# A linear-attention and feed-forward kernel: v loaded in long rows with its ones written by GpSimd, and an order planned for later landings

## The chip, the cores and the metric

The kernel runs on 1 core of one Trainium2 chip. The metric is device time in microseconds, the median of several executions. TensorE (PE) does the matmuls, VectorE (DVE), ScalarE (ACT) and GpSimd (POOL) the rest, and the queue of SyncE (SP) issues most transfers.

## The reference

The inputs are q, k, v of 8 batches x 8 heads x 576 positions x 64, float32, a projection `w_phi` (64 x 128), and the weights of two feed-forward parts, which arrive as float64 and are converted on the chip. What is computed, for each head:

```
phi(x) = [exp(p), exp(-p)]   with p = x @ w_phi - max|x @ w_phi|     (256 features)
kv = phi(k)^T @ v ,  z = sum over positions of phi(k)
attention = (phi(q) @ kv) / (phi(q) @ z + 1e-6)
```

The heads are then joined to x (8 x 576 x 512). The first feed-forward part mixes each position with the one before it (`mu`), and gives sigmoid(xr @ w_r) * (relu(xk @ w_k)^2 @ w_v). The second gives (sigmoid(causal convolution of 5 taps) * (x @ w_val)) @ w_out.

## The kernel before

**Attention.** The 64 pairs of batch and head are taken in 16 rounds n of four heads each; a round is two steps, so there are 32 steps j. In each step two heads (`ab` = 0, 1) go through: projection of q and k on TensorE (`q_proj`, `k_proj`, L615); the largest absolute value and its subtraction on VectorE (L621, L623); exponentials on ScalarE, for q behind a transposition (`turn`, L680, L684); the sums of kv (`kv`, L721); the numerators (`num`, L755); the scaling by the reciprocal of the denominator, on GpSimd and VectorE (`scale`, L772 to L781); and the transposition back (`back`, L795), after which each round is stored to the scratch tensor xs. The last 64 of the 576 positions (the tails) are treated once in a round for all heads.

The z sums come free with kv: v lies in SBUF with 65 columns for each head and block of 128 positions, the 65th a column of ones. Two buffers, `vts[0]` and `vts[1]`, take turns. Their ones are written once, at the start (L576); the load of round n (`load_v`, L599) writes the 64 columns between them, 16 pieces of 256 bytes for each partition, and two small transfers bring the tails. All three go through SP (`load`, L391).

**Conversion of the weights.** 28 pieces of weights are loaded as float64 bits, narrowed to float32 by ScalarE and VectorE (`narrow`, L411 to L425), combined into the seven products of a Strassen scheme, and split by GpSimd into a high and a low part (`part_two`, L463 and L457). The parts of w_k stay in SBUF. All the others go into one of two staging buffers ("ql", shown as dd in the trace) and from there to the scratch tensor ws in HBM; the next cast into a buffer waits until the store from it has landed. This work is spread over the attention steps (`convert`, from FROM to TO).

**Feed-forward parts.** Behind the attention `moe` runs the two parts batch by batch with matmuls of 128x128 against 288 columns (L897), fetching the weights from ws in units (`fetch_unit`, L903), 1 MB each as a rule.

**What sets the order.** The order of the instructions is worked out at build time by a planner, `Order` (the class before the helper functions of durations). Every task has an engine, an estimated duration, what it reads and writes, and a due time in units of a step (the table `T`: `load_v=-1.8` means 1.8 steps ahead of the step itself). For each engine the planner goes through its tasks in the order of due times and takes the first that can start as soon as the engine is free, or, if there is none, the one that can start earliest. A transfer is reckoned to be done DMA_START + bytes / DMA_RATE + DMA_END after it is issued (and behind the transfers before it); what reads it cannot start in the plan before that. For TensorE, tasks of the same array shape are preferred to a due time of EARLY steps ahead. PORT is added where GpSimd and VectorE both work on SBUF. On the chip each engine then runs its list in order, and waits on semaphores where something isn't ready.

Of the kernel before, what the change touches and what calls it, by code (L numbers as in the profile page):

```python
# [25 lines left out]
def pattern(bits):  # L26
# [3 lines left out]
LEAST, MOST = pattern((896 + 128) << 20), pattern(((1150 + 128) << 20) | 0xFFFFF)  # L30


T = dict(load_q=-1.89, load_k=-2.75, load_v=-1.8, tails=-1.0, q_proj=-1.5, k_proj=-1.05, turn=-0.6, sums=-0.5,
         num=0.4, back=1.4, finish=1.9, convert=1.09)
FROM, TO = 1, 27

LAST = ("pj", "qp", "kv")

AFTER_PE = 0.2
AFTER = 0.08  # L40
SAME = 0.04
PORT = 0.28
TAIL = {"ACT": 0.1, "DVE": 0.08, "POOL": 0.05}
DMA_START = 1.3
DMA_END = 1.0
DMA_RATE = 350e3


KV = 0.117
ENTER = {"rows": 0.2, "columns": 0.14, "all": 0.15}  # L50
SOON, EARLY = 0.6, 0.8
SPLIT, FORK_R = 8, False


# [80 lines left out]
class Order:  # L135
# [6 lines left out]
    def add(self, eng, dur, fn, r=(), w=(), new=(), at=None, dma=0, split="all"):  # L142
        t = {"eng": eng, "dur": dur, "fn": fn, "deps": set(), "at": self.now if at is None else at,
             "id": len(self.tasks), "new": list(new), "dma": dma, "end": None, "split": split,
             "bufs": set()}
        t["port"] = eng == "POOL" or eng == "DVE" and dur > 0.3 and not any(
            isinstance(x, Buf) and x.tag in self.banks.most for x in itertools.chain(r, w))
        for x in r:
            t["deps"].update(self.last_write.get(x, ()))
        for x in w:  # L150
            t["deps"].update(self.reads.pop(x, ()))
            t["deps"].update(self.last_write.get(x, ()))
        for x in r:
            self.reads.setdefault(x, []).append(t["id"])
        for x in w:
            self.last_write[x] = [t["id"]]
        for b in new:
            self.queue.setdefault(b.tag, []).append((b, t["id"]))
        for x in itertools.chain(r, w):
            b = x[0] if isinstance(x, tuple) else x  # L160
            if isinstance(b, Buf):
                b.users.append(t["id"])
                t["bufs"].add(b)
        t["deps"].discard(t["id"])
        self.tasks.append(t)

    def run(self):
# [44 lines left out]
        while left:  # L212
# [36 lines left out]
            if t["port"]:  # L249
                other = busy.get("POOL" if t["eng"] == "DVE" else "DVE", 0.0)  # L250
                if at < other - 0.05:
                    t["dur"] += PORT
                    if t["eng"] == "DVE":
                        free["POOL"] += PORT
                        busy["POOL"] += PORT
                busy[t["eng"]] = at + t["dur"]
            free[t["eng"]] = at + t["dur"] - TAIL.get(t["eng"], 0.0)
            t["end"] = at + t["dur"]
            if t["dma"]:
                dma_free = max(dma_free, at + DMA_START) + t["dma"] / DMA_RATE  # L260
                t["end"] = dma_free + DMA_END
            todo[t["eng"]].remove(t)
# [30 lines left out]
def build(ctx, tc, qt, kt, vv, wphi, mu, wk, wr, wv, wval, cw, wout, out):  # L293
    nc = tc.nc
# [30 lines left out]
    for i, side in enumerate(("left", "right")):  # L325
        p = sides[i].enter_context(tc.tile_pool(name=f"s{i}", bufs=1, space=bass.MemoryType.PSUM, side=side))
# [14 lines left out]
    add = G.add  # L341
# [4 lines left out]
    def view(page, off, shape, dtype=F32, own=F32):  # L346
        n = 1
        for k in shape[1:]:
            n *= k
        a, names = pages[page][:, off:off + n], "abcd"[:len(shape) - 1]  # L350
        if len(names) > 1:
            a = a.rearrange(f"p ({' '.join(names)}) -> p {' '.join(names)}", **dict(zip(names, shape[1:])))
        return a if dtype == own else a.bitcast(dtype)
# [34 lines left out]
    def load(dst, src, nbytes, r=(), w=(), new=(), at=None, by="SP"):  # L388

        q = {"SP": nc.sync, "ACT": nc.scalar}[by]  # L390
        add(by, 0.62 if by == "SP" else 0.1, lambda: q.dma_start(out=dst(), in_=src()), r=r, w=w, new=new, at=at,  # L391
            dma=nbytes)
# [166 lines left out]
    vts = [view(*PLACE[f"v{i}0"], [128, 2048]) for i in range(2)]  # L559
    vtok = [Buf(f"v{i}", lambda i=i: vts[i]) for i in range(2)]  # L560
# [10 lines left out]
        load(lambda a=a: wph[64 * a:64 * a + 64], lambda: wphi, 32768, w=[("wph", a)], by="ACT")  # L571
    G.now = -5.0
    for i in range(2):
        def ones(t=vts[i]):
            nc.gpsimd.memset(t[:, 1040:1300], 0.0)
            nc.gpsimd.memset(t[:, 0:1040].rearrange("p (k x) -> p k x", x=65)[:, :, 64:65], 1.0)  # L576
            for p in range(2):
                for ab in range(2):
                    c = 1104 + 65 * p + 130 * ab
                    nc.gpsimd.memset(t[64 * p:64 * p + 64, c:c + 1], 1.0)  # L580

        add("POOL", 1.0, ones, w=[(vtok[i], "ones")], new=[vtok[i]])

    ks, qs, st = {}, {}, {}

# [13 lines left out]
    def load_v(n):  # L599
        vt, vk = vts[n % 2], vtok[n % 2]  # L600
        gate = ["first"] if n else []
        load(lambda: vt[:, 0:1040].rearrange("p (k x) -> p k x", x=65)[:, :, 0:64], lambda: vv[n, :, 0:16], 524288,
             r=gate, w=[(vk, 0)])
        for p in range(2):
            def dst(p=p):
                a = 1040 + 65 * p
                return vt[64 * p:64 * p + 64, a:a + 260].rearrange("p (a x) -> p a x", x=130)[:, :, 0:64]
            load(dst, lambda p=p: vv[n, 64 * p:64 * p + 64, 16:18], 32768, r=gate, w=[(vk, "t", p)])

    def project(bs, x, cols, at):  # L610

# [672 lines left out]
    def due(t, fn, *args):  # L1284
        events.append((t, len(events), fn, args))
# [8 lines left out]
    for j in range(NP):  # L1294
        n, p = divmod(j, 2)
        st[j] = {}
        if p == 0:
            due(j + T["load_q"] if n else -8.0, load_t, n, qs, qt, "q")
            due(j + T["load_k"] if n else -7.0, load_t, n, ks, kt, "k")
            due(j + T["load_v"] if n else -6.0, load_v, n)  # L1300
            due(j + T["tails"], tails, j)
        due(j + T["q_proj"], q_proj, j)
        due(j + T["k_proj"], k_proj, j)
        if p == 0:
            due(j + T["turn"] + 0.4, turn_tails, n)
        for ab in range(2):
            due(j + T["turn"] + 0.3 * ab, turn, j, ab)
        due(j + T["sums"], kv, j)
        for ab in range(2):
            due(j + T["num"] + 0.3 * ab, num, j, ab)  # L1310
        due(j + T["num"] + 0.5, scale, j)
        due(j + T["back"], back, j)
        if p:
            due(j + T["finish"], finish, n)
        if j == 5:
            due(j + 0.5, small)
    for p in pieces:
        j = FROM + (TO - FROM) * spent / total
# [50 lines left out]
```

## Time and profile before

| | |
|---|---|
| median of 3 executions | 962.9 us (962.85 to 969.19) |
| the profiled execution, own time | 967.21 us |
| its span, first to last instruction | 965.4 us |
| TensorE busy | 936.1 us (97%), mean granted clock 0.995 |
| VectorE, ScalarE, GpSimd busy | 831.9, 686.2, 200.9 us |
| packets of the DMA engines | 110490, of these 42912 under 512 B |
| sums of kv of the last step begin at | about 307 us; the first matmul of L897 at 313 us |

The span is that of one execution. Busy time of TensorE includes matmuls that overlap each other in the pipeline. A wait is idle time of an engine, put down to what ended it. The rows that the prediction uses stand further down.

### The profile page before, as it was taken

How to read it: one execution, taken by the hardware profiler on the slowest of the kernel's cores; microseconds unless marked ns; L12 is line 12 of the kernel's file. 1: busy time of each engine (PE TensorE's matmuls, PEld its weight loads, DVE VectorE, ACT ScalarE, POOL GpSimd, SP SyncE). 2: the span in 40 equal slices, each digit the busy share in tenths (PEclk: the TensorE clock that was granted, in tenths of full speed). 3: DMA queues.
4: the chain of work that ended last, by engine and by line, in shares of the span. 5: the costliest groups of instructions: out<-in, count | busy, mean ns of one | idle time of the engine just before them, and what ended most of it. 6: DMA issues, size and time to landing. Idle time of an engine off the chain costs nothing.

```text
span 965.4 us, 26969 instructions
## 1 busy us (share of the span) xinstructions
PE 936.1 (97%) x11264; PEld 908.0 (94%) x11264; DVE 831.9 (86%) x1276; ACT 686.2 (71%) x1253; POOL 200.9 (21%) x346
## 2 busy tenths in 40 slices
PE   7999999999899999999999999999999999999997
PEld 6998988888798999999999999999999999999997
DVE  4899988789888699979978988997997898899695
ACT  4677676668677898767957957876895795787453
POOL 0258978677673000000000000000000000000000
PEclk9999999999999999999999999999999999999999
DMA  8566599889975566488478567748837866754784
GB/s 229 167 180 192 171 272 281 262 255 277 302 262 182 173 236 229 148 310 282 146 262 282 208 237 268 248 157 304 289 135 263 279 211 241 271 193 165 275 304 140
DMA packets 110490, 224.14 MB, mean 232 GB/s; under 512 B 42912, under 2 KB 67872, under 8 KB 97312
## 3 DMA queue, kind: packets, MB, share of 16 engines
q1 hardware_dynamic: 101072, 212.32, 65.9%
q10 hardware_dynamic: 9296, 10.09, 3.0%
q8 instruction: 89, 1.46, 0.6%
q14 instruction: 33, 0.27, 0.1%
HBM read 186.74 MB, written 35.65 MB: 230 GB/s over the span
## 4 chain that ended last, share of the span: by engine, by line
PE 56%; DVE 13%; DMA 13%; ACT 9%; POOL 5%; issue 3%; SPq 1%; ACTq 0%; DVEq 0%; POOLq 0%
PE c L897 43%; DMA ws<-dd 6%; DMA out<-y 5%; PE b L721 4%; PE b L755 4%; PE b L615 3%; DVE ops L373 3%; POOL dd L457 2%; DVE k L866 2%; ACT y L875 2%; ACT g L875 1%; PE b L680 1%; DVE g L869 1%; ACT ops L875 1%; POOL dd L463 1%
## 5 line engine op out<-in xcount | busy, mean ns | idle before, releaser
L897 PE MATMUL c<-ops,u 128*128 128x288 f32 x1968 | 276.7, 296 | 5.7 <-DVE ops L373 3.9
L897 PEld LDWEIGHTS c<-ops,u 128*128 128x128 f32 x1968 | 266.3, 188 | 8.7 <-DVE ops L373 5.9
L897 PE MATMUL c<-ops,wkt 128*128 128x288 f32 x1344 | 179.6, 295 | 0.0
L897 PEld LDWEIGHTS c<-ops,wkt 128*128 128x128 f32 x1344 | 178.3, 188 | 0.2
L621 DVE TENSOR_REDUCE dd<-b 128x4 f32<-128x512 f32 (+1 forms) x160 | 94.6, 624 | 19.0 <-PE b L615 18.2
L869 DVE SCALAR_TENSOR_TENSOR g<-x,cwt,g 128x576 f32<-128x576 f32 x128 | 101.8, 811 | 0.0
L875 ACT ACTIVATE ops<-k 128x576 fp32r<-128x576 f32 x96 | 65.2, 680 | 46.3 <-PE c L897 43.2
L373 DVE TENSOR_TENSOR ops<-k,ops 128x576 fp32r<-128x576 f32 x96 | 71.6, 755 | 24.3 <-ACT ops L875 23.9
L615 PE MATMUL b<-wph,ops 64*128 64x128 f32 x1152 | 82.1, 286 | 2.2 <-DMA ops<-in_kt 1.5
L755 PEld LDWEIGHTS b<-g,y 128*64 128x64 f32 x2176 | 68.5, 140 | 12.1 <-issue 5.8
L755 PE MATMUL b<-g,y 128*64 128x65 f32 x2176 | 74.6, 226 | 5.3 <-issue 3.1
L684 ACT ACTIVATE y<-b 128x512 f32<-128x512 f32 x128 | 69.8, 606 | 13.9 <-PE b L680 13.7
L615 PEld LDWEIGHTS b<-wph,ops 64*128 64x128 f32 x1152 | 70.7, 190 | 9.2 <-issue 3.3
L875 ACT ACTIVATE k<-k 128x576 f32<-128x576 f32 x98 | 64.0, 681 | 2.4 <-DVE k L866 2.1
L875 ACT ACTIVATE sp<-c 128x576 f32<-128x576 f32 x50 | 32.5, 649 | 41.0 <-PE c L897 41.0
L370 ACT ACTIVATE x<-b 128x260 f32<-128x260 f32 (+3 forms) x96 | 38.8, 424 | 27.4 <-PE b L755 20.6
L623 DVE TENSOR_TENSOR k<-b,dd 128x512 f32<-128x512 f32 (+1 forms) x84 | 49.3, 612 | 0.0
L897 PE MATMUL c<-y,u 128*128 128x288 f32 x336 | 48.0, 295 | 0.0
L897 PE MATMUL c<-y,xf 128*128 128x288 f32 x336 | 46.8, 295 | 0.0
L897 PEld LDWEIGHTS c<-y,u 128*128 128x128 f32 x336 | 45.7, 188 | 0.0
L897 PEld LDWEIGHTS c<-y,xf 128*128 128x128 f32 x336 | 45.3, 188 | 0.0
L875 ACT ACTIVATE k<-c 128x576 f32<-128x576 f32 x64 | 41.3, 645 | 4.5 <-PE c L897 4.3
(148 smaller groups left out, 1791.0 us busy)
## 6 DMA issues: line engine op xcount, KB each, us to landing
u<-ws SPq DMA_DIRECT2D x86, 1024.0 KB, 5.4
xf<-ws SPq DMA_DIRECT2D x16, 1024.0 KB, 5.4
ws<-dd SPq DMA_DIRECT2D x28, 512.0 KB, 5.6
dd<-ws SPq DMA_DIRECT2D x24, 512.0 KB, 5.9
ot<-ws SPq DMA_DIRECT2D x20, 512.0 KB, 5.9
xs<-x SPq DMA_DIRECT2D x16, 576.0 KB, 4.4
xx<-xs SPq DMA_DIRECT2D x8, 1152.0 KB, 7.7
out<-y ACTq DMA_DIRECT2D x32, 288.0 KB, 5.4
```

Source lines behind the costliest of these rows:

```text
L370: act(out=out, in_=x, func=AF.Copy)
L373: eng.tensor_tensor(out=out, in0=x, in1=hi.bitcast(F32), op=ALU.subtract)
L457: nc.gpsimd.tensor_tensor(out=o[:, c], in0=a[:, c], in1=b[:, c], op=op)
L615: mm(out=bs[ab][:, (at + i) * 128:(at + i + 1) * 128], lhsT=x[r, c:c + 128], rhs=wph[r], start=True, stop=True)
L621: add("DVE", t_dve(128 * n), lambda: nc.vector.tensor_reduce(out=m[:, 0:n, 0], in_=b3[:, 0:n], axis=AX.X, op=ALU.max, apply_absolute_value ...
L623: add("DVE", t_dve(128 * n), lambda: tt(out=d[0](), in0=b3[:, 0:n], in1=m[:, 0:n].to_broadcast([128, n, 128]), op=ALU.subtract), r=[b, m], ...
L684: add("ACT", t_act(512), lambda half=half: act(out=e[:, ab, half, :], in_=b[:], func=AF.Exp, scale=-1.0 if half else 1.0), r=[b], w=[(e, a ...
L721: mm(out=b[y, o:o + 65], lhsT=lhs[:, y], rhs=vt[:, a:a + 65], start=(k == 0), stop=(c == 3), skip_group_check=True)
L755: mm(out=b[rows, at:at + 65], lhsT=lhs, rhs=a[:, o:o + 65], start=(k == 0), stop=(half == 1), skip_group_check=True)
L869: add("DVE", d_time(n) + 0.06, lambda: stt(out=out(), in0=x(), scalar=scalar(), in1=y(), op0=ALU.mult, op1=ALU.add), r=r, w=w)
L875: act(out=out(), in_=x(), func=func, **more)
L897: mm(out=o[:, half, 0:TB], lhsT=a, rhs=mov[b][c], start=first and k == 0, stop=last and k == n - 1, skip_group_check=True)
```

## The change

The array of v is made with a 65th zero column for each block, so that a partition's 16 blocks are one row of 1040 floats, in HBM as in SBUF; it is loaded by one transfer of long rows, which also overwrites the column of ones with zeros. GpSimd writes the ones again behind each load (`ones(n)`, a memset of 128x16, a task of its own with due time `ones=-1.23`), 16 times instead of twice. The two transfers of the tails keep their shape. Besides, the planner's constants are changed: transfers are taken to land 1.5 us later (DMA_END), PORT is a little larger, EARLY about half; the conversions begin at step 0 rather than 1 and end at 27.43 rather than 27; and the projection of k, the load of v and the transposition back are due earlier. The due time of `turn` changes by 0.008.

```diff
-T = dict(load_q=-1.89, load_k=-2.75, load_v=-1.8, tails=-1.0, q_proj=-1.5, k_proj=-1.05, turn=-0.6, sums=-0.5,
-         num=0.4, back=1.4, finish=1.9, convert=1.09)
-FROM, TO = 1, 27
+T = dict(load_q=-1.89, load_k=-2.75, load_v=-2.03, tails=-1.0, q_proj=-1.5, k_proj=-1.505, turn=-0.592, sums=-0.5, num=0.4, back=1.049, finish=1.9, convert=1.09, ones=-1.23)
+FROM, TO = 0, 27.43
-PORT = 0.28
+PORT = 0.321
-DMA_END = 1.0
+DMA_END = 2.5
-SOON, EARLY = 0.6, 0.8
+SOON, EARLY = 0.6, 0.405
@@ at the start
-        def ones(t=vts[i]):
+        def tails_of(t=vts[i]):
             nc.gpsimd.memset(t[:, 1040:1300], 0.0)
-            nc.gpsimd.memset(t[:, 0:1040].rearrange("p (k x) -> p k x", x=65)[:, :, 64:65], 1.0)
@@ def load_v(n)
-        load(lambda: vt[:, 0:1040].rearrange("p (k x) -> p k x", x=65)[:, :, 0:64], lambda: vv[n, :, 0:16], 524288,
-             r=gate, w=[(vk, 0)])
+        load(lambda: vt[:, 0:1040], lambda: vv[n, :, 0:1040], 532480, r=gate, w=[(vk, 0)])
@@
+    def ones(n):
+        vt, vk = vts[n % 2], vtok[n % 2]
+        add("POOL", 0.12, lambda: nc.gpsimd.memset(vt[:, 0:1040].rearrange("p (k x) -> p k x", x=65)[:, :, 64:65], 1.0),
+            w=[(vk, 0)])
@@ for each step j, of the first step of a round
             due(j + T["load_v"] if n else -6.0, load_v, n)
+            due(j + T["ones"] if n else -4.0, ones, n)
@@ kernel()
+    padded = np.pad(main, ((0, 0), (0, 0), (0, 0), (0, 1)))
-        "vv": np.concatenate([main, tail], axis=2),
+        "vv": np.concatenate([padded.reshape(16, 128, 1040), tail.reshape(16, 128, 128)], axis=2),
```

## Rows read from the trace of the kernel before

**Rows 1.** Stretches: length, engines' busy us, granted clock, DMA share, GB/s.

```profile
100.00:120.00 20.00, 20.00 (x455) 18.25 (x452) 19.76 (x37) 14.15 (x32) 19.09 (x29) 1.00 0.55 162
...
400.00:500.00 100.00, 99.69 (x751) 99.46 (x750) 85.91 (x117) 66.77 (x110) 0.00 (x0) 1.00 0.69 245
```

**Rows 2.** Waits of TensorE, 313 to 966 us: total us, times, longest.

```profile
PE c L897 <- DVE ops L373: 3.9, 6, 1.1
```

**Rows 3.** Timeline of TensorE, three sums of kv: start, duration, tiles.

```profile
16.21 1.76 PE L721 MATMUL b<-u,k 128*64 128x65 f32 x48 [1.77 <-POOL omm L1289]
...
123.77 1.62 PE L721 MATMUL b<-u,k 128*64 128x65 f32 x48
...
301.07 1.81 PE L721 MATMUL b<-u,k 128*64 128x65 f32 x48 [0.60 <-ACT k L657]
```

**Rows 4.** Line L391, stores to the scratch tensor: issuing ns, first and last start.

```profile
L391 SPq DMA_DIRECT2D ws<-dd x36: 359/377/1640, 124.7 to 292.5; - x36
```

**Rows 5.** Waits of GpSimd, 20 to 300 us, same columns.

```profile
POOL dd L463 <- DMA ws<-dd: 28.8, 15, 4.0
```

**Rows 6.** Timeline of GpSimd at one such wait: start, duration, [idle before].

```profile
136.46 0.40 POOL L463 CAST dd<-ot 128x256 fp32r<-128x256 f32 x1 [3.61 <-DMA ws<-dd]
136.81 0.61 POOL L777 TENSOR_TENSOR ot<-x,g 128x256 f32<-128x256 f32 x1
```

**Rows 7.** Waits of TensorE, 16 to 313 us, same columns.

```profile
PE b L795 <- POOL ot L777: 5.1, 4, 1.9
PE b L755 <- issue: 3.1, 2, 1.8
...
PE b L721 <- POOL omm L1289: 1.8, 1, 1.8
...
PE b L795 <- POOL ot L781: 0.8, 1, 0.8
...
PE b L795 <- POOL x L777: 0.7, 2, 0.5
```

**Rows 8.** The page, DMA issues: count, KB each, median us to landing.

```profile
u<-ws SPq DMA_DIRECT2D x86, 1024.0 KB, 5.4
...
ws<-dd SPq DMA_DIRECT2D x28, 512.0 KB, 5.6
...
u<-in_vv SPq DMA_DIRECT2D x16, 512.0 KB, 5.2
```

**Rows 9.** Stretches behind a load of v issued at 177.53.

```profile
176.00:180.00 4.00, 2.32 (x25) 2.00 (x27) 1.63 (x5) 2.23 (x6) 3.75 (x8) 0.80 0.78 216
180.00:184.00 4.00, 4.00 (x90) 3.93 (x88) 1.05 (x4) 3.20 (x9) 4.00 (x8) 0.77 1.01 188
184.00:188.00 4.00, 4.00 (x103) 3.75 (x100) 3.97 (x8) 1.88 (x5) 2.89 (x6) 1.00 1.01 382
```

**Rows 10.** Timeline of the SP queue: start, duration of issuing, tiles, count.

```profile
81.38 2.12 SPq L391 DMA_DIRECT2D u<-in_vv  x3
...
85.02 0.33 SPq L391 DMA_DIRECT2D ops<-in_qt  x1
```

**Rows 11.** Lines L576 and L772: duration ns min/median/max, first and last start.

```profile
L576 POOL MEMSET u<- x2: 125/130/136, 1.5 to 2.2; 128x16 f32 x2
...
L772 POOL TENSOR_SCALAR dd<-x x31: 236/254/845, 24.4 to 308.7; 128x8 f32<-128x8 f32 x16, 128x10 f32<-128x10 f32 x15
```

**Rows 12.** The chain that ended last, 0 to 340 us: start, duration, line, count.

```profile
57.43 2.02 PE b L755 x64
59.44 1.99 PE b L615 x32
...
73.33 1.08 PE b L755 x32
74.42 1.09 PE b L615 x16
```

**Rows 13.** Waits of the SP queue, 0 to 300 us.

```profile
SPq L391 <- PE b L721: 34.7, 9, 7.7
```

More of the change, by code (lines that the diff above doesn't have):

```diff
@@ L580, in ones @@
                     nc.gpsimd.memset(t[64 * p:64 * p + 64, c:c + 1], 1.0)
-        add("POOL", 1.0, ones, w=[(vtok[i], "ones")], new=[vtok[i]])
+        add("POOL", 1.0, tails_of, w=[(vtok[i], "ones")], new=[vtok[i]])
     ks, qs, st = {}, {}, {}
@@ L607, in dst @@
                 return vt[64 * p:64 * p + 64, a:a + 260].rearrange("p (a x) -> p a x", x=130)[:, :, 0:64]
-            load(dst, lambda p=p: vv[n, 64 * p:64 * p + 64, 16:18], 32768, r=gate, w=[(vk, "t", p)])
+            load(dst, lambda p=p: vv[n, 64 * p:64 * p + 64, 1040:1168].rearrange("p (a x) -> p a x", x=64), 32768,
+                 r=gate, w=[(vk, "t", p)])
+    def ones(n):
+        vt, vk = vts[n % 2], vtok[n % 2]
+        add("POOL", 0.12, lambda: nc.gpsimd.memset(vt[:, 0:1040].rearrange("p (k x) -> p k x", x=65)[:, :, 64:65], 1.0),
+            w=[(vk, 0)])
     def project(bs, x, cols, at):
```

## The prediction

> **What bounds the kernel now.** I read the page first, then stretches, then TensorE's timeline, then the waits. The page has TensorE busy for nearly all of the span, which says little: the figure mixes two stages. In the second, from about 313 us to the end (the two feed-forward parts), 100 us hold 99.69 us of matmuls [rows 1], and the longest group of TensorE's waits there is 3.9 us in all [rows 2]. There is almost nothing to win, and the change edits nothing there but the planner's idea of landings. In the first stage (attention, with the weights converted beside it) the reader should use a milestone, not busy time. The sum of kv of each even step is one: it starts at 16.21 us for step 0, 123.77 for step 12 and 301.07 for step 30 [rows 3]. The first six pairs of steps take (123.77 - 16.21) / 6 = 17.9 us each, the last nine (301.07 - 123.77) / 9 = 19.7. If the later ones went at the early pace, 9 x (19.70 - 17.93) = 15.9 us would be won. That is the room.
>
> What slows the late pairs? From 124.7 us on the converted weights are stored to the scratch tensor in HBM, 36 times [rows 4], and GpSimd may write the next piece only when the store from that buffer has landed. GpSimd stood 28.8 us in 15 such waits [rows 5], 1.9 us each. The attention's own scaling (L777, L781) is queued behind: at 136.46 it waited 3.61 us for a landing and only then did the scaling that the transposes of L795 need [rows 6]. TensorE waited 5.1 + 0.8 + 0.7 = 6.6 us for that scaling [rows 7]. The cause is legible in the planner: it reckons a transfer of 512 KB to end 1.3 + 524288/350e3 + 1.0 = 3.8 us after its issue, and the stores took 5.6 [rows 8]. So it puts GpSimd's instruction where it believes the store done, about 1.8 us early.
>
> **The change part by part.**
>
> *Landings (DMA_END 1.0 to 2.5), with PORT, EARLY, FROM and TO.* The planned end becomes 5.3 us, against 5.6 for a store and 5.2 for a load of v [rows 8]. Of a mean wait of 1.9 us the later landing covers 1.5, or about three quarters, if the planner finds other GpSimd work for that time; it takes the first task that is ready, so scaling can pass a cast whose buffer isn't free. Three quarters of 6.6 us is -5.0. Bounds: -6.6 (all of it) and 0 (the wait moves to another instruction). The pieces of conversion are spread over 27.43 periods instead of 26 and begin one earlier, which thins the work by 5%; that eases the same waits and I count it once. PORT only makes the planner count GpSimd and VectorE as a little slower when both run.
>
> *The load of v.* Before, its rows land as pieces of 256 bytes, 65 floats apart: 128 x 16 = 2048 pieces for each of 16 loads. Its data show as a DMA share of 1.01 at 188 GB/s, while the next 4 us move 382 GB/s at the same share [rows 9]. So 512 KB hold all engines for about 2.8 us and would for 1.4 in long rows: 16 x 1.4 = 22 us of DMA time go, in a stage of 300. SP also spends at least 2.12 us on issuing the three v transfers, against 0.33 for one of q in long rows [rows 10]; I estimate 0.33 + 2 x 0.4 after. On TensorE this is worth what waited for it: "issue" 3.1 us in two waits, where the profile shows nothing that was waited for, and 1.8 us at the first kv sum [rows 7]. I take -1.5, about one of the two issue waits; bounds -4.9 and 0. The start gains little: the first kv sum now needs the landing and then a memset.
>
> *The ones.* Two memsets at the start go, sixteen come: 14 x 0.130 [rows 11] = 1.8 us more on GpSimd, each waiting for the landing of v before it, and ahead of one kv sum in two. Cover: GpSimd's own waits of 28.8 us [rows 5]; cost 0. If the cover is gone, and each stretches as L772's longest did, to 0.845 us [rows 11], that is 16 x 0.845 = 13.5 us of GpSimd, and at the present rate of 6.6 us of TensorE wait per 28.8 it costs +3.1. Queued behind a waiting memset are the casts, subtractions and the scaling. The short duration was measured with VectorE idle. The Trainium skill, "SBUF — State Buffer", section "Who interferes with whom", says that a GpSimd instruction which only writes SBUF doesn't contend with a VectorE one reading two SBUF inputs, but that VectorE's two-port modes lock it out. By that rule the stretching would come from the conversions' tensor_scalar alone and the cost stay near 0; no run here shows a memset beside VectorE's work.
>
> *Steps that move.* The projection of k goes 0.455 of a period earlier (about 4 us), so that its 16 matmuls stand beside q's 16, and its four centring instructions on VectorE and four exponentials on ScalarE come earlier with it; the load of k is due more than a period ahead, so nothing new is awaited. Sixteen and sixteen apart take 2 x 1.09 us, thirty-two together 1.99 [rows 12]: 0.2 saved per join, and the row of 16 stands for some twenty in TensorE's timeline, so ten joins, -2.0. Against that, EARLY halves how far the planner reaches ahead for work of the same shape; a num of 64 split in two costs 2 x 1.08 - 2.02 = 0.14 [rows 12], and 16 new splits +2.2. I take -1.0; bounds -2.0 and +2.2. The transposes back go 0.35 of a period earlier: they depend on the scaling, and gain only if that is early too. The load of v goes 0.23 earlier (2 us), ahead of q's on SP. It cannot be issued before the sum of kv that last read its buffer, for which SP stood 34.7 us [rows 13], so q's load would stand behind it; q isn't among TensorE's longer waits now, cost 0.
>
> *The feed-forward stage.* A fetch of 1 MB took 5.4 us [rows 8]; it was planned at 5.3 and is now at 6.8, later than real. Planned too late costs only if TensorE is given something worse meanwhile. I take 0; bounds -3.9 (all of [rows 2]) and +8.8, the longest wait there, 1.1, once for each of eight batches.
>
> **Sum:** -5.0 - 1.5 + 0 - 1.0 + 0 = -7.5 us. The profiled execution took 967.2, 4.3 above the median of 962.9. Of this 1.7 us is the clock: 0.80 and 0.77 over two stretches of 4 us [rows 9], a mix of 2.4 and 1.2 GHz, behind a TensorE idle of 1.9 us that ended with L777 [rows 7]. If that wait goes, 967.2 - 7.5 - 1.7 = 958.0 for an execution like that one; against the median, 962.9 - 7.5 = 955.4.
>
> **The rivals.**
> - *The late pairs reach the early pace.* The 6.6 us are only what TensorE's rows name; pairs lose 15.9 in all, part of it in matmuls regrouped around late work. If landings were the one cause, the time is 962.9 - 15.9 = 947.0. For it: the slowdown sets in with the stores. Against: the early pairs have conversions too and no stores.
> - *No change.* The pace is set by the work of the conversions: in one early stretch VectorE has 19.76 of 20 us and GpSimd 19.09 [rows 1]; a wait taken from one instruction reappears at the next. 962.9, within 3 us. Against it: GpSimd's 28.8 us idle.
> - *GpSimd waits for v instead (slower).* The memset stands in GpSimd's order where the plan has the landing at 5.3 us, and v lands at 5.2: no slack. SP stands behind the kv sum for up to 7.7 us [rows 13], so a TensorE that runs late delays the load, the memset, the scaling and TensorE again. If 8 of the 15 later loads cost TensorE its longest such wait, 1.9 us [rows 7], and the stores' gain is eaten, 962.9 + 15.2 = 978.1. It decides when loads are issued over 1 us later than planned relative to GpSimd. Against: the planner knows SP's queue, and v now lands sooner.
>
> **How the numbers follow.** Forecast 0.36, early pace 0.28, no change 0.24, slower 0.12. The predicted time is 955.4. The range of 944 to 969 takes in the forecast with its bounds, the early pace and no change, and leaves out the slower rival and something below the early pace. About 1%, 9.6 us, is what a measurement can tell from no change. Faster by more: the early pace and a quarter of the forecast, 0.28 + 0.09 = 0.37; slower 0.12; within 0.51.
>
> **What would show it.** Packets under 512 B should fall by 16 x 2048 = 32,768; GpSimd's wait for stores to under 12 us; TensorE's waits on the scaling from 6.6 to about 2; the way from step 12 to step 30 from 177.3 to some 170 us; the three v transfers should issue in under 1.5 us. It is wrong if GpSimd waits long for the landing of v, if the steps' pace stays while the waits change names, or if the feed-forward stage becomes longer.

## The result, and the profile after

The changed kernel is faster: 958.4 us (median) against 967.5 of the kernel before, timed beside it; the ratio is 0.991, with a 95% interval of 0.988 to 0.994. By that ratio it is 8.8 us less (6.1 to 11.4). The forecast was 7.5 us less.

The page of the changed kernel: span, busy time, packets.

```profile
span 955.8 us, 27000 instructions
...
PE 933.7 (98%) x11264; PEld 906.8 (95%) x11264; DVE 831.3 (87%) x1276; ACT 690.6 (72%) x1253; POOL 204.3 (21%) x360
...
DMA packets 79770, 224.27 MB, mean 235 GB/s; under 512 B 10144, under 2 KB 35104, under 8 KB 66592
```

Its own execution took 957.6 us against 967.2, so the two profiles are 9.6 us apart, about as far as the medians, and may be compared. TensorE's busy time fell by 2.4 us, its idle time by 7.2. The packets under 512 B fell by 32,768, exactly as many as there were pieces of 256 bytes.

The timeline of TensorE (start, duration, line, tiles, count, idle before it; the lines are three further down than before, L724 for L721, L900 for L897): the first projection, the sums of kv of steps 0, 12 and 30, and the first matmul of the feed-forward stage.

```profile
9.80 5.00 PE L618 MATMUL b<-wph,ops 64*128 64x128 f32 x56 [4.68 <-DMA ops<-in_kt]
...
18.88 1.76 PE L724 MATMUL b<-u,k 128*64 128x65 f32 x48
...
123.27 1.62 PE L724 MATMUL b<-u,k 128*64 128x65 f32 x48
...
292.65 1.62 PE L724 MATMUL b<-u,k 128*64 128x65 f32 x48
...
305.36 2.65 PE L900 MATMUL c<-ops,wkt 128*128 128x288 f32 x18
```

Set beside [rows 3], this says where the 9.6 us are. The first sum of kv starts at 18.9 instead of 16.2: **2.7 lost** at the start. Steps 0 to 12 take 104.4 instead of 107.6: 3.2 won. Steps 12 to 30 take 169.4 instead of 177.3: **7.9 won**, 18.8 us a pair instead of 19.7. From step 30 to the first L900, 0.4 is lost (12.7, where before it was 12.3), and from there to the end 650.4 us remain instead of 652.0: 1.6 won.

Where the 7.9 us of steps 12 to 30 come from is seen in these two stretches, before and after (length, then busy us of TensorE, weight loads, VectorE, ScalarE, GpSimd; granted clock, DMA share, GB/s):

```profile
123.77:301.07 177.30, 165.43 (x3646) 150.62 (x3645) 149.91 (x280) 122.44 (x273) 127.01 (x216) 0.99 0.87 270
...
123.27:292.65 169.38, 166.37 (x3688) 151.51 (x3686) 153.13 (x283) 124.26 (x273) 126.21 (x219) 1.00 0.83 270
```

TensorE was idle for 177.3 - 165.4 = 11.9 us of the one and for 3.0 us of the other, and about as long busy. Before, 1.7 us of the busy time was lost to the clock as well (0.80 and 0.77 in [rows 9]); after, the clock was granted in full.

TensorE's waits of 16 to 313 us (total us, times, longest): the four that are listed.

```profile
PE b L758 <- issue: 2.9, 2, 1.5
PE b L618 <- issue: 1.6, 2, 0.9
PE b L683 <- DVE sp L626: 1.4, 1, 1.4
PE b L724 <- issue: 1.4, 2, 0.8
```

No wait for GpSimd is left among them, against three kinds of waits for its scaling and 6.6 us in [rows 7]. What heads the list is "issue". GpSimd's own waits of 20 to 300 us, for the landing of stores and of v:

```profile
POOL dd L462 <- DMA ws<-dd: 10.6, 11, 2.1
...
POOL u L610 <- DMA u<-in_vv: 6.0, 3, 5.3
```

The wait for stores fell from 28.8 us [rows 5] to 10.6, although a store took a little longer to land (count, KB, median us to landing):

```profile
ws<-dd SPq DMA_DIRECT2D x28, 512.0 KB, 6.2
...
u<-in_vv SPq DMA_DIRECT2D x16, 520.0 KB, 4.0
```

A store took 6.2 us, against 5.6 in [rows 8]: so it isn't the stores that became faster; what is left is that GpSimd comes to them later, with other work ahead of it. A load of v lands in 4.0 us instead of 5.2.

### The profile page after: what moved, and what is told of

It is laid out like the page before. It is cut to its first block, busy times and chain, and to the rows that moved or that the text cites. A ratio compares the mean times of both kernels' runs of the same rounds, so it can differ in the third digit from the quotient of the medians.

```text
span 955.8 us, 27000 instructions
## 1 busy us (share of the span) xinstructions
PE 933.7 (98%) x11264; PEld 906.8 (95%) x11264; DVE 831.3 (87%) x1276; ACT 690.6 (72%) x1253; POOL 204.3 (21%) x360
## 4 chain that ended last, share of the span: by engine, by line
PE 88%; DVE 5%; ACT 4%; DMA 2%; issue 1%; ACTq 0%; DVEq 0%
PE c L900 58%; PE b L724 8%; PE b L618 8%; PE b L758 8%; PE b L683 4%; PE b L798 2%; DVE ops L372 1%; ACT ops L878 1%; DMA out<-y 1%; DVE x L869 1%; DMA ops<-in_kt 1%; ACT y L878 0%; ACT x L878 0%; ACT g L878 0%; PE b L696 0%
## 5 line engine op out<-in xcount | busy, mean ns | idle before, releaser
L900 PE MATMUL c<-ops,u 128*128 128x288 f32 x1968 | 275.5, 295 | 4.1 <-DVE ops L372 2.5
L900 PEld LDWEIGHTS c<-ops,u 128*128 128x128 f32 x1968 | 266.2, 188 | 6.1 <-DVE ops L372 3.4
L900 PE MATMUL c<-ops,wkt 128*128 128x288 f32 x1344 | 180.0, 295 | 0.7 <-ACT c L1021 0.7
L900 PEld LDWEIGHTS c<-ops,wkt 128*128 128x128 f32 x1344 | 178.3, 188 | 1.1 <-ACT c L1021 0.9
L687 ACT ACTIVATE y<-b 128x512 f32<-128x512 f32 x128 | 69.9, 599 | 13.4 <-PE b L683 12.3
L900 PE MATMUL c<-y,u 128*128 128x288 f32 x336 | 48.0, 294 | 0.0
L900 PE MATMUL c<-y,xf 128*128 128x288 f32 x336 | 46.8, 295 | 0.0
L900 PEld LDWEIGHTS c<-y,u 128*128 128x128 f32 x336 | 45.7, 188 | 0.0
L900 PEld LDWEIGHTS c<-y,xf 128*128 128x128 f32 x336 | 45.3, 188 | 0.0
```

The costliest lines, as they stand in the source:

```text
L687: add("ACT", t_act(512), lambda half=half: act(out=e[:, ab, half, :], in_=b[:], func=AF.Exp, scale=-1.0 if half else 1.0), r=[b], w=[(e, a ...
L900: mm(out=o[:, half, 0:TB], lhsT=a, rhs=mov[b][c], start=first and k == 0, stop=last and k == n - 1, skip_group_check=True)
```

## The experiments

Each ratio is to the kernel before, on the same chip, with its interval; the us are worked out on 966. The last column is TensorE's busy time in the 193 us from 120 to 313 (profiled execution); where the attention ends early, the last few us of it belong to the feed-forward stage.

| kernel | ratio | us | GpSimd waits for stores | TensorE busy, 120 to 313 |
|---|---|---|---|---|
| before | 1 | 0 | 28.8 | 180.6 |
| PORT alone (control) | 1.0036 (1.0012 to 1.0060) | +3.5 | 30.8 | 180.7 |
| DMA_END alone | 0.9999 (0.9973 to 1.0024) | -0.1 | 20.3 | 178.3 |
| layout and memsets alone | 0.9971 (0.9946 to 0.9996) | -2.8 | 20.2 | 182.7 |
| changed kernel without DMA_END | 0.9963 (0.9939 to 0.9988) | -3.6 | 23.9 | 187.0 |
| DMA_END and due times | 0.9935 (0.9914 to 0.9956) | -6.3 | 16.6 | 184.9 |
| DMA_END, FROM, TO, EARLY, PORT | 0.9893 (0.9868 to 0.9918) | -10.3 | 18.4 | 189.3 |
| all planner constants, old layout | 0.9901 (0.9873 to 0.9930) | -9.6 | 12.6 | 187.6 |
| changed kernel | 0.9909 (0.9882 to 0.9937) | -8.8 | 10.6 | 188.5 |

**The layout and its memsets alone.** All constants as before, `ones=-1.23`.

```diff
-        load(lambda: vt[:, 0:1040].rearrange("p (k x) -> p k x", x=65)[:, :, 0:64], lambda: vv[n, :, 0:16], 524288,
-             r=gate, w=[(vk, 0)])
+        load(lambda: vt[:, 0:1040], lambda: vv[n, :, 0:1040], 532480, r=gate, w=[(vk, 0)])
...
+            due(j + T["ones"] if n else -4.0, ones, n)
```

> The new layout of v and the sixteen memsets alone, with the landings, due times and other constants of the kernel before (ones due at -1.23). If the late landings in the plan carry the gain (theory A), this stays within 4 us of before: GpSimd still waits some 25 us for stores (28.8 before), and TensorE some 5 to 7 us for the scaling. If the lighter load of v carries it (theory B), it is 6 to 10 us faster than before, and the waits for stores fall by half because the stores land sooner. If the memset is what hurts, GpSimd waits over 10 us for v and the time is 5 us or more above before.

2.8 us faster, with the edge of the interval (0.9996) nearly at 1. It fits theory A by its size, but the waits for stores fell to 20.2, more than expected, and TensorE's for the scaling to 3.6 us, where 5 to 7 were expected. GpSimd waited 5.8 us for v, well under the 10 that would have marked the memset as harmful.

**The later landing alone.**

```diff
-DMA_END = 1.0
+DMA_END = 2.5
```

> The kernel before with DMA_END 2.5 in place of 1.0 and nothing else. Theory A: 4 to 8 us faster than before; GpSimd's waits for stores fall from 28.8 to under 14 us and TensorE's for the scaling from 6.6 to under 3. Theory B: within 3 us of before. A third theory (C), that any new order differs by as much: no tie between the waits and the time.

Theory A fails in its plain form: 0.9999, and the interval leaves out the 4 to 8 us. GpSimd's waits for stores fell to 20.3, where under 14 were expected. Yet the mechanism is there. TensorE's waits, the three "issue" rows and the longest that is left for the scaling:

```profile
PE b L721 <- issue: 3.5, 2, 2.5
PE b L615 <- issue: 2.9, 2, 2.2
PE b L755 <- issue: 2.4, 3, 1.0
...
PE b L795 <- POOL ot L777: 0.7, 1, 0.7
```

and GpSimd's for stores:

```profile
POOL dd L463 <- DMA ws<-dd: 20.3, 12, 3.5
```

The wait for the scaling of L777 fell from 5.1 us [rows 7] to 0.7. In its place stand 8.8 us of "issue", against 3.1, and the clock. Two rows of TensorE's timeline, each behind an idle of 2 us or more:

```profile
164.73 3.40 PE L755 MATMUL b<-g,y 128*64 128x65 f32 x64 [2.00 <-ACT g L370]
...
301.03 0.39 PE L721 MATMUL b<-u,u 128*64 128x65 f32 x6 [2.52 <-issue]
```

Stretches of 4 us (length, then busy us of TensorE, weight loads, VectorE, ScalarE, GpSimd; granted clock, DMA share, GB/s) around them:

```profile
164.00:168.00 4.00, 3.27 (x64) 3.21 (x64) 2.97 (x4) 3.56 (x8) 2.62 (x4) 0.64 1.03 367
297.00:301.00 4.00, 1.51 (x51) 1.37 (x47) 3.17 (x4) 2.33 (x4) 3.17 (x4) 1.00 0.98 361
301.00:305.00 4.00, 3.97 (x30) 3.57 (x31) 0.03 (x1) 2.84 (x7) 0.28 (x1) 0.59 0.07 23
```

Behind those idles the clock stood at 0.64 and 0.59 over 4 us each, so half speed (1.2 GHz) for most of it: 4 x 0.36 + 4 x 0.41 = 3.1 us lost. One wait was removed, and others, with the clock they cost, took its place in this execution. The "issue" waits are for TensorE's own instructions, as the last section shows, and which matmuls they strike changes with the order.

**All planner constants, the old layout.** The first half of the change's diff (T, FROM, TO, PORT, DMA_END, EARLY) on the kernel before.

> All constants of the planner as after the change, but v loaded in pieces of 256 bytes and its ones written twice at the start, as before. Theory A: nearly the whole gain, 6 to 9 us faster than before. Theory B: within 3 us of before. The remainder to the changed kernel (8.8 us faster) is what the layout of v is worth under the new plan; I expect 1 to 3 us.

0.9901: the whole gain, without the layout. In the trace its matmuls, and VectorE's and ScalarE's instructions, stand in the changed kernel's order, one by one; GpSimd's too, but for the memsets. So the order carries the gain. The layout's own 1 to 3 us didn't show.

**The changed kernel without the later landing.**

```diff
-DMA_END = 2.5
+DMA_END = 1.0
```

> The changed kernel with DMA_END back at 1.0. Theory A: 5 to 9 us slower than the changed kernel, so within 4 us of before; GpSimd waits over 20 us for stores again (10.6 in the changed kernel), and longer for v (6.0 there), since the memset is planned 1.5 us too early. Theory B: within 3 us of the changed kernel, 6 to 9 us faster than before.

5.2 us slower than the changed kernel, as theory A had it. GpSimd's waits:

```profile
POOL dd L462 <- DMA ws<-dd: 23.9, 17, 4.0
...
POOL u L610 <- DMA u<-in_vv: 4.7, 4, 2.8
```

Those for stores are back at 23.9; those for v did not grow (4.7, against 6.0), so that part of the expectation is wrong.

**The layout under one and the same order.** The main load in pieces again, with the planner given the same number of bytes: the lists of TensorE, VectorE, ScalarE and GpSimd are the changed kernel's, memsets included.

```diff
-        load(lambda: vt[:, 0:1040], lambda: vv[n, :, 0:1040], 532480, r=gate, w=[(vk, 0)])
+        load(lambda: vt[:, 0:1040].rearrange("p (k x) -> p k x", x=65)[:, :, 0:64], lambda: vv[n, :, 0:16], 532480, r=gate, w=[(vk, 0)])
...
```

> The changed kernel with its own order of instructions on TensorE, VectorE, ScalarE and GpSimd, sixteen memsets included, but the main part of v again in pieces of 256 bytes. It separates layout from order. If the long rows are worth what the prediction took (1.5 us and shorter landings), this is 1 to 4 us slower than the changed kernel, and GpSimd waits over 8 us for v (6.0 in the changed kernel). The rival: the long rows gain nothing under this order, because at the start they hold up the first load of k (TensorE waited 4.7 us for it in the changed kernel, 1.6 in the one with the new constants and v in pieces); then this one starts its first kv sum 2 to 3 us earlier than the changed kernel and its time is equal within 2 us.

0.9916 (0.9882 to 0.9950) against 0.9909: equal as far as the intervals tell, which reach some 3 us either way and do not rule out the 1.5 us that the prediction took. What the rival named is in the timeline (the first projection and the first sum of kv):

```profile
6.76 5.39 PE L618 MATMUL b<-wph,ops 64*128 64x128 f32 x56 [1.63 <-DMA ops<-in_kt]
...
15.84 1.76 PE L724 MATMUL b<-u,k 128*64 128x65 f32 x48
```

TensorE waited 1.6 us for k and not 4.7, and the first sum of kv starts at 15.8, not 18.9. From there to the end it needs 939.6 us, the changed kernel 936.9. So between these two profiles the one with long rows loses 3.0 us at the start and wins 2.7 later. GpSimd had no wait for v of the kind expected here (over 8 us): none is listed.

**The control.** PORT 0.28 to 0.321 on the kernel before.

> The kernel before with PORT 0.321 in place of 0.28: a control, since it hardly changes what the planner believes and yet reorders most rows of every engine. If any new order of this planner differs by several us (theory C), this is 3 us or more off before, either way. If the gain has named causes (theory A), it is within 3 us of before, and GpSimd's waits for stores stay at 25 us or more.

3.5 us slower (1.2 to 5.8), above 3, so theory C has a part: one new order that should mean nothing moved the time by some 3.5 us. GpSimd's wait for stores stays:

```profile
POOL dd L463 <- DMA ws<-dd: 30.8, 16, 4.1
```

Differences of up to that size between two of these kernels can't be put down to the edit.

**Two repairs of the start.** q's projection first in step 0; and, apart from it, the first main load of v from ScalarE's queue, behind the first load of k.

```diff
-        due(j + T["k_proj"], k_proj, j)
+        due(j + (T["k_proj"] if j else -1.49), k_proj, j)
```

> The changed kernel with the projection of q ahead of that of k in step 0 alone (due -1.49 for k there). In the changed kernel k goes first and TensorE waits 4.7 us for its load. Expected: the first kv sum starts 1.5 to 2.5 us earlier than 18.9 us; the time 1 to 2 us below the changed kernel, if the new order behind it is no worse. Theory C: the difference is swamped by the new order, and it may be slower by some us.

```diff
-        load(lambda: vt[:, 0:1040], lambda: vv[n, :, 0:1040], 532480, r=gate, w=[(vk, 0)])
+        load(lambda: vt[:, 0:1040], lambda: vv[n, :, 0:1040], 532480, r=gate, w=[(vk, 0)], by="SP" if n else "ACT")
```

> The changed kernel with the main part of the first v load issued from ScalarE's queue behind the first k load, so that k lands first; the order of GpSimd stays nearly the same. If the long rows of v hold up k's landing, TensorE's first wait for k falls from 4.7 us to under 2.5, the first kv sum starts 2 us or more earlier, unless it then waits for v; the time is 1 to 3 us below the changed kernel. If the k load is slow for another reason, the wait stays above 4 us.

The first gave 0.9905 (0.9870 to 0.9939), its first sum of kv at 15.2 us; the second 0.9906 (0.9875 to 0.9937). In the timeline of the second:

```profile
6.82 5.10 PE L618 MATMUL b<-wph,ops 64*128 64x128 f32 x56 [1.69 <-DMA ops<-in_kt]
...
15.90 1.76 PE L724 MATMUL b<-u,k 128*64 128x65 f32 x48
```

The wait for k is 1.7 us instead of 4.7, as it would be if v in long rows on SP's queue had held up k on ScalarE's; the last section says why that isn't shown. The time of each is less than 1 us below the changed kernel's ratio, where 1 to 2 and 1 to 3 were expected; the intervals don't resolve it.

**Due times or spread.** To find which constants go with the landing, the kernel before with DMA_END 2.5 and, in one kernel, the new T (with `k_proj`, `back`, `load_v` moved), in the other FROM, TO = 0, 27.43, EARLY = 0.405 and PORT = 0.321.

> The kernel before with DMA_END 2.5 and the new due times (k's projection beside q's, back and the load of v earlier), v in pieces and FROM, TO, EARLY and PORT as before. If the due times together with the landings carry the gain, 5 us or more faster than before, with TensorE's waits of 16 to 313 us under 7 us in all. If the conversions' earlier start and wider spread (FROM, TO) are needed, it stays within 4 us of before.

> The kernel before with DMA_END 2.5 and FROM, TO, EARLY and PORT as after the change, but the old due times and v in pieces. The complement of the run beside it: if the spread of the conversions with the landings carries the gain, 5 us or more faster than before; if the due times are needed, within 4 us of before. If both runs gain 3 to 6 us, the parts add; if neither does, only all together do.

The second has the whole gain, 0.9893. The first has some 70% of it, 0.9935, though TensorE's waits come to 11.6 us, where under 7 were expected. They don't add. In the second, the sum of kv of step 0 and the last numerators, and below them the last numerators before:

```profile
13.78 1.76 PE L721 MATMUL b<-u,k 128*64 128x65 f32 x48 [0.68 <-issue]
...
305.81 0.64 PE L755 MATMUL b<-g,x 128*64 128x65 f32 x16
...
312.43 0.64 PE L755 MATMUL b<-g,x 128*64 128x65 f32 x16
```

TensorE's longest waits,

```profile
PE b L755 <- issue: 3.2, 2, 2.3
PE b L721 <- issue: 2.6, 2, 1.6
PE b L693 <- ACT y L684: 0.7, 1, 0.7
```

and GpSimd's for stores:

```profile
POOL dd L463 <- DMA ws<-dd: 18.4, 13, 3.3
```

GpSimd still waits 18.4 us for stores, hardly less than with DMA_END alone, but nothing on TensorE hangs on them any more: besides "issue" no wait reaches 1 us, and the last numerators are done 6.6 us earlier than before.

**k's projection back at its old place** in the changed kernel (`k_proj=-1.05`).

> The changed kernel with k's projection due at -1.05 as before. If its move beside q's is worth the joins that I counted (1 to 2 us net), 1 to 4 us slower than the changed kernel, except that the start, where q goes first again, gives back some 2 us. If the move is what removed TensorE's waits, those for the exponentials of k and for the scaling come back, 3 us or more in all, and it is 4 us or more slower.

0.9909 (0.9888 to 0.9930), the same as the changed kernel: nothing of the move shows in the time, within some 3 us. Its first sum of kv starts at 14.5 us, 4.4 earlier than in the changed kernel, and the rest of the way gives it back.

**Both repairs of the start together.**

> The changed kernel with q's projection first in step 0 and the first main load of v behind the first load of k on ScalarE's queue: both repairs of the start. Each alone moved the first kv sum from 18.9 to some 15.5 us and came out at 0.9905 of before. Together I expect TensorE's wait for k under 1 us, the first kv sum at 14 to 15.5 us, and 10 to 13 us below before. If the start is only hidden elsewhere, it equals each alone.

0.986 (0.983 to 0.989), 953.3 us against 966.2: 13.5 us below before, the fastest of all. The first projection, the sum of kv of step 0, the end of attention:

```profile
5.05 2.82 PE L618 MATMUL b<-wph,ops 64*128 64x128 f32 x40
...
13.71 1.76 PE L724 MATMUL b<-u,k 128*64 128x65 f32 x48 [0.58 <-issue]
...
299.53 2.64 PE L900 MATMUL c<-ops,wkt 128*128 128x288 f32 x18
```

and all that is left of TensorE's waits of 16 to 313 us:

```profile
PE b L724 <- issue: 1.9, 1, 1.9
PE b L758 <- issue: 1.8, 1, 1.8
```

It beats the kernel before clearly. Against the changed kernel the two intervals just touch, and they were not timed side by side, so that it beats that one too is likely and not proved. Nor is its lead on the kernel with q first alone (0.9905): the four engines' orders are the same in both, the intervals overlap, and the two profiled executions took 954.0 and 953.9 us.

## Why the prediction was right, and where it was right by luck

The forecast (-7.5 us, 0.992) lies inside the measured interval. The predicted 955.4 us stood on the median of three executions of the kernel before, 962.9; the eleven beside the changed kernel gave 967.5 and 958.4. For the profiled execution, with 1.7 us for the clock, the prediction came to 958.0, and it took 957.6. The gain lies where it was put: TensorE's waits for the scaling are gone, the late steps quicker (169.4 us; 170 was said), the stage behind them nearly unchanged. But the terms are not what I made them. Nor does the range, 944 to 969, take in the forecast with its bounds, as I wrote: these add up to -17.4 and +14.1, which is 945.5 to 977.0.

- *Landings with their companions: -5.0 taken, -8 to -10 measured.* This term was mis-sized. I priced it by the 6.6 us that TensorE's rows put down to GpSimd [rows 7], with that as the bound. With DMA_END, FROM, TO, EARLY and PORT it was -10.3, with the due times as well -9.6, and under the order of the changed kernel, layout undone, -8.1. TensorE's idle time of 16 to 313 us, of all kinds, was 297 - 281.9 = 15.1 before and is 297 - 290.9 = 6.1 in the changed kernel (the stretch before, then after, in the columns used above):

```profile
16.00:313.00 297.00, 281.94 (x6357) 258.52 (x6358) 256.66 (x477) 211.12 (x474) 197.02 (x323) 0.99 0.76 234
...
16.00:313.00 297.00, 290.90 (x6442) 266.87 (x6443) 265.73 (x493) 223.16 (x488) 202.23 (x342) 1.00 0.73 239
```

  The waits for ScalarE went too. Nor is DMA_END the cause by itself, as I had reasoned from the stores: alone it gave nothing, and under the new constants it is worth 5.2 us. Eight kernels have both the later landing and the wider spread, and all gained 8 us or more. They have only four orders of the matmuls, though: the changed kernel's, which the old layout, the pieces and v behind k share (0.9901 to 0.9916, so an order repeats to within 1.5 us); that with q first; and those of two more. Of the five kernels without both, the nearest (DMA_END and due times) gained 6.3, less than the control's 3.5 us away from them. So that DMA_END needs companions is shown; which of them, FROM and TO, EARLY or the due times, was not separated. Nor was it tested whether it acts by way of the stores: the constant holds for every transfer.
- *The long rows of v: -1.5 taken, nothing measured that clears the noise* (0.7 us under one and the same order). The mechanism was right in part: 32,768 packets fewer, landings of 4.0 us. But the price was taken from two "issue" waits, and nothing ties these to v: like all such waits behind 16 us they end behind a packet of TensorE's instructions (last section), and under one order of the matmuls they come to 5.9 us with long rows and to 5.7 and 6.9 with pieces. The issue of three v transfers didn't fall under 1.5 us: at best it took 1.6, several times over 2, against 2.12 in [rows 10]. And I gave the start no cost, where the changed kernel's profile loses 2.7 us to the load of k.
- *The ones: cost 0, as taken.* All sixteen memsets of the changed kernel (duration ns min/median/max, first and last start):

```profile
L610 POOL MEMSET u<- x16: 121/128/318, 10.0 to 269.4; 128x16 f32 x16
```

  Fifteen of the sixteen ran beside an instruction of VectorE, and the median is 128 ns, as in [rows 11] without it. The rule of the Trainium skill, "SBUF — State Buffer", section "Who interferes with whom", that a GpSimd instruction which only writes isn't held up by VectorE's two-input ones, agrees: two ran wholly beside one that reads two SBUF inputs (L420, L424) and took 127 ns each. The longest, 318 ns, ran beside a tensor_scalar of the conversions (L413), the one place where I had expected stretching; another beside the same instruction took 128. The longest in the timeline of both engines:

```profile
128.07 0.42 DVE L413 TENSOR_SCALAR xf<-xf 128x512 f32<-128x512 f32 x1
...
128.24 0.32 POOL L610 MEMSET u<- 128x16 f32 x1
```

  GpSimd waited 6.0 us for v after 20 us, 5.3 of it at the load of round 1, when its next instruction had to wait for ScalarE until ten us later anyway, and no wait of TensorE from 16 us on is put down to it. That disposes of the slower rival.
- *Steps that move: -1.0 taken, nothing seen* when k's projection was put back, which is a whole new order and tells no more than some 3 us. The cost that I missed is at the start: k due 0.005 ahead of q puts k first in step 0 too, where q is there earlier.
- *The feed-forward stage: 0 taken, -1.6 between the two profiles*, less than the new order of the control moved the time.

So -7.5 came near -8.8 by luck: one term was too small by half, and of the other two that were taken nothing shows. The rival of the early pace was too bold: 18.8 us a late pair, not 17.9. The rival of no change fails, for GpSimd's waits did not move to another name on TensorE, except with DMA_END alone, where just that happened.

## What to carry to other kernels

Where a written order decides, give the planner the landing times that the trace shows, but judge them together with the spread of the work that is to fill the wait: here the landing alone moved the idle to other causes. Price such a change by all idle time of the bounding engine in the stage, and run a control with a meaningless change of order to learn the grain, here 3.5 us by a single one. And look at the first microseconds apart: two small edits there moved the first sum of kv from 18.9 to 13.7 us, though what that is worth in the time (4.7 us between kernels that weren't timed side by side) isn't proved, and two due times 0.005 apart had put the wrong load first.

## What the runs showed of the hardware

**That long rows on one queue hold up another queue's load is not shown.** With the first v in long rows on SP's queue, the first two loads of k (256 KB each) on ScalarE's landed after 7.3 us in the changed kernel (median) and TensorE started at 9.8; with v in 256-byte pieces under the same order after 5.5 us, start at 6.8. But over all profiles the two groups overlap: 5.4, 5.5, 5.5, 6.1 and 7.3 us with long rows, 5.5 (three times), 5.7, 5.7, 5.8 and 6.5 with pieces. Only v issued behind k lies below both, with 5.2 and 4.1. So the 7.3 us belongs to that execution, and the 3 us at its start may too. The Trainium skill, "DMA: Bandwidth & Descriptors", section "Queues, rings and completion order", says that each DMA engine goes round between the queues a packet at a time; no run here shows what longer rows leave to the other queue.

**TensorE's "issue" waits end behind a packet of its instructions.** They fall in the middle of a group of equal matmuls, with nothing named that they waited for. The page lists a DMA queue q8, "instruction", with 89 packets of 16 KB in an execution (packets, MB, share of the engines' time). One such packet of the changed kernel starts between 23.0 and 23.1 us, then TensorE stands still from 24.05 to 25.46 (stretch in the columns used above, then its next matmuls):

```profile
q8 instruction: 89, 1.46, 0.6%
...
q8 instruction: 1, 0.02, 58.4%
...
24.05:25.45 1.40, 0.00 (x1) 0.00 (x0) 1.40 (x4) 0.47 (x1) 0.00 (x0) 1.00 0.15 56
...
25.46 0.85 PE L758 MATMUL b<-g,y 128*64 128x65 f32 x21 [1.41 <-issue]
```

The DMA share is 0.15 there, so the wait does not need busy DMA engines. With DMA_END alone, a packet that starts between 298.6 and 298.7 is followed by the longest such wait, at a share of 1.01:

```profile
q8 instruction: 1, 0.02, 60.0%
...
298.50:301.00 2.50, 0.01 (x1) 0.00 (x0) 2.50 (x3) 0.83 (x2) 2.50 (x3) 1.00 1.01 355
```

The fourteen profiles have 67 "issue" waits of over 0.2 us between 16 and 313 us. Every one ends 2.2 to 2.9 us after a packet of q8 started (median 2.4), at DMA shares from 0 to over 1, and 13 of them at under 0.5. (Of those before 16 us some have no such packet and stay unexplained.) And their places are regular: in the changed kernel they come behind 221, 2634, 4286, 4667, 5048 and 6446 matmuls, and in every profile the distances are multiples of 127, to within ten; 11,264 matmuls to 89 packets are one packet for 127. This reads as TensorE coming to the seam between two packets before the next is there. The three other kernels with the changed kernel's order have waits at the same four seams from 2634 to 5048, whatever the layout or queue of v. Some fifty packets start in that stretch and two to eight of them cost time, 2.2 to 8.8 us in all; what makes these few late isn't shown, and no experiment moved the seams alone. A new order moves other matmuls to the seams, which can be a part of the grain; in the control, though, these waits grew by 0.8 us alone (3.1 to 3.9).
